# Two heads' last key tiles in one 256-column score product: a pre-norm block of segmented memory attention and GEGLU on one Trainium2 core

## The chip, the cores and the metric

The kernel runs as one program on one core of a Trainium2 chip. The metric is the time of one execution on the device in microseconds (us), the median of several runs; lower is better. The core's engines work side by side, each through its own queue in program order: TensorE (PE: matrix products, with the weight loads as a row of their own, PEld), VectorE (DVE), ScalarE (ACT), GpSimd (POOL), and SyncE (SP), which here issues all DMAs. An instruction waits in its engine's queue until the semaphores it names are set, and whatever stands behind it waits too. The matrix products write into eight accumulation banks in PSUM, each 128 partitions by 512 float32.

## What is computed

A transformer block over 2048 rows of 512 features, in float32: layer norm, attention in four segments of 512 rows with a compressive memory between the segments, residual, layer norm, GEGLU feed-forward (inner width 1376), residual. There are 32 heads of width 16.

```python
phi = lambda t: jnp.where(t > 0, t + 1.0, jnp.exp(t))
for s in range(N):                                  # N = 4 segments of L = 512 rows
    qs, ks, vs = q[:, :, s], k[:, :, s], v[:, :, s]
    logits = jnp.einsum("bhqd,bhkd->bhqk", qs, ks) * scale + mask
    p = _softmax(logits, axis=-1)
    a_dot = jnp.einsum("bhqk,bhkd->bhqd", p, vs)
    pq = phi(qs)
    num = jnp.einsum("bhld,bhde->bhle", pq, M)
    den = jnp.einsum("bhld,bhd->bhl", pq, z)[..., None] + 1e-6
    outs.append(g * (num / den) + (1.0 - g) * a_dot)
    pk = phi(ks)
    M = M + jnp.einsum("bhld,bhle->bhde", pk, vs)
    z = z + jnp.einsum("bhld->bhd", pk)
...
h = x + _A_ref(_layernorm(x, axis=-1), A_wq, A_wk, A_wv, A_wo, A_beta)
h2 = h + _B_ref(_layernorm(h, axis=-1), B_w_gate, B_w_up, B_w_down)   # (gelu(g) * u) @ w_down
```

The mask adds -1e9 where the key's index is below the query's, so each query attends to itself and to later keys of its segment. In the transposed scores (keys on partitions, queries along the columns) key tile `kb` of 128 keys needs the queries from `kb*128` on in the kernel's order of tiles: 512, 384, 256 and 128 columns for `kb` 0 to 3.

## The kernel before

**A planner writes the order.** The kernel's text describes operations with an engine, a modelled duration, the values they read and write (`Val`) and a due number `prio`. `Sched.run` simulates the five queues with these durations and a table of latencies between engines (`LAT`), takes at each step the operation that can start first (among those within 0.059 us the lowest `prio`), gives it buffers from pools, and emits its instructions. So the order in every queue is fixed when the program is built, and it follows from the modelled durations and from the table `DUE`, which shifts the due numbers of each unit's stages by up to four steps either way. A pool (`Pool_`) passes its buffers on to the pool named by `then` when nobody waits for them any more; `fifo=True` serves its values in the order of their creation.

**Attention.** A unit is a pair of a chunk of eight heads and a segment, 16 in all; each has two halves of four heads, so there are 32 passes `Q`. A product in full float32 precision is made of three products of split operands (`SPLIT`): a high part in float32r and the rest. `qkv` projects queries and keys (L576), splits them, and DMAs scatter the parts into stacks: `stq` (128 partitions, head pair `p`, 512 queries) and `stk` (128 partitions, `p`, `a`, 512 keys). Two heads share a pair `p`; head `a` of the two has its own 64 partitions in `stk[:, p, a]`, and the other 64 partitions are zero, so that one product over 128 partitions gives the scores of one head. `pass_a` computes scores with queries on partitions (L754), and the row maxima from them on VectorE (L764); these go by a DMA (L792, `stq<-mx`) into a row of `stq`, and with it a product of stacks gives scores less their maximum. `pass_b` computes the transposed scores (L809), the exponentials on ScalarE (L813), sets the masked triangle to zero on GpSimd (L817, `affine_select`), and multiplies by the values (L838, `accum`, four heads side by side in the array).

In `pass_b` the function `bank(parts)` fills one score bank with the parts `(head, column, key tile)`, runs one exponential over all 512 columns and the selections. A pass has ten banks: four heads with key tile 0 (512 columns), four heads with key tiles 1 and 3 (384 and 128 columns), and two banks with key tile 2 of two heads each. `accum` is called twice, for key tiles (0, 1) and (3, 2). The score banks are two (`PB`), the probabilities' buffers ten (`pt1` and `pt`).

**Start.** `ln1(0)` loads four row tiles, takes statistics (L483), an inverse square root by three Newton steps on VectorE (L488 to L499, twelve small instructions), normalizes four tiles (L504), transposes them on PE (L530, chunk by chunk of the features) and splits them (L539 on ScalarE, L540 on VectorE). Seventeen transposes of the last raw row tile (L555) keep PE at work before. `c_stk` fills the stacks with ones and zeros (L411 on ScalarE, L414 on GpSimd).

**Feed-forward.** It runs over two halves of the rows, `p` = 0 and 1, each 1024 rows as two sets of 512. The products are formed by a Strassen scheme of seven (`ffn`, L1082), whose operands `B[p]` come from `ln2` on both sets; `down` multiplies by the down weights (L1143). `B[p]` has fourteen operand tiles from the pool `PBL`, and those of the second half take over those of the first. For `B[1]` the rows are loaded again (L1189) into `PROW`, a pool of four row buffers that both sets use.

Of the kernel before, what the change touches and what calls it, by code (L numbers as in the profile page):

```python
# [242 lines left out]
def infini_geglu(ctx: ExitStack, tc: tile.TileContext, x, wq, wk, wv, wo, beta,  # L243
# [29 lines left out]
    def dma(prio, fn, ins, outs, kb=256, dur=None, **k):  # L273
        return S.op("SP", dur or (0.4 if kb == 256 else 0.64), prio, fn, ins, outs, lat=kb / 290, **k)
# [28 lines left out]
    PSQ = Pool_(stq_t, fifo=True, then=Parts(1, PBL, PBL, Parts(2, *[PHH] * 2), Parts(2, *[PHH] * 2)))  # L303
    PHL = Pool_(slots("hl", 3), fifo=True, then=Parts(1, FIN, Parts(2, *[PHH] * 2), Parts(2, *[PHH] * 2)))
    PROW = Pool_(many("row", 4, [P, D]), fifo=True)
    PRAW = Pool_(many("raw", 3, [P, D]), fifo=True)
# [7 lines left out]
    PPQ = Pool_(many("pq", 2, [P, D]), then=PC)  # L314
# [16 lines left out]
    PLN = Pool_(many("ln", 6, [P, 4]))  # L331
# [51 lines left out]

    vone, vq0, vk0, vv0 = Val(), [Val() for _ in stq_t], [Val() for _ in stk_t], [Val() for _ in va_t]
# [6 lines left out]
    def c_fill():  # L391
        for i, t in enumerate(stq_t):
            pool(0.93, -4.2 + 0.1 * i, lambda t=t: nc.gpsimd.memset(t.bitcast(F32), 0.0),
                 [vcalm[0]] if i > 1 else [], [vq0[i]])
# [53 lines left out]
    def layer_norm(prio, rows, dst, off=False, keep=None, acq=None, done=(), behind=(), scratch=None):  # L448
# [15 lines left out]
        def m_():  # L464
            return sc.t[:, 8:12] if scratch else mv.t[:, :, 0]
# [775 lines left out]
```

## Time and profile before

| | |
|---|---|
| runs (median, lowest to highest) | 847.04 us, 844.33 to 847.7 |
| the profiled execution, its span | 844.19 us, 842.5 us |
| mean granted clock of TensorE | 0.994 |
| instructions in the span | 15436 |
| DMA traffic in the span | 103.52 MB, mean 123 GB/s |

The span goes from the first to the last instruction; the time of the execution has some 1.7 us around it. The profile gives for each engine the time in which at least one of its instructions was under way; matrix products are pipelined, so their durations overlap (a single product of 512 columns is shown with about 0.4 us, though they follow each other faster). Groups of instructions are named by line, engine, operation and `out<-in` with the names of the buffers. As buffers are passed on between pools, a name tells where a buffer was first used, not what it holds: `stk` in the feed-forward stage is an operand tile. In the rows of the timeline stand the start, the length, what was done how often, and in brackets the idle time before it with what ended it.

### The profile page before, as it was taken

The numbers are of one execution on the slowest core, as the hardware profiler recorded it, in microseconds if no ns is written. First come the engines' busy times: TensorE is split into PE (matmuls) and PEld (weight loads), VectorE is DVE, ScalarE is ACT, GpSimd is POOL, SyncE is SP. The second block draws the span as 40 slices with busy tenths as digits, with TensorE's granted clock in tenths as the row PEclk, the third lists the DMA queues.
The fourth block names the chain that finished last, engine by engine and source line by source line (L and its number), as shares of the span: only waits on it lengthen the run. The fifth ranks groups of instructions, "written<-read, shape, count | busy, mean of one in ns | idle before, by whom it ended". The sixth has DMA issues, their size and how long they took to land.

```text
span 842.5 us, 15436 instructions
## 1 busy us (share of the span) xinstructions
PE 815.5 (97%) x4773; PEld 636.7 (76%) x4773; DVE 614.6 (73%) x1847; ACT 511.3 (61%) x966; POOL 493.9 (59%) x813
## 2 busy tenths in 40 slices
PE   5999999999999999999899999999999999999998
PEld 4887686776777777867576677878888777887886
DVE  7877789787976877769987864665567887656565
ACT  6765657678865656663675752684467664645551
POOL 6433436444444544545656895897696666778750
PEclk9999999999999999999999999999999999999999
DMA  6435445556456565356454654421113611212102
GB/s 225 113 97 141 133 132 144 162 162 170 124 139 177 138 182 136 104 152 194 131 177 141 217 182 146 127 86 53 54 57 100 209 45 38 65 49 63 50 1 100
DMA packets 71750, 103.52 MB, mean 123 GB/s; under 512 B 14324, under 2 KB 24884, under 8 KB 71668
## 3 DMA queue, kind: packets, MB, share of 16 engines
q1 hardware_dynamic: 71668, 102.54, 41.8%
q8 instruction: 38, 0.62, 0.3%
q14 instruction: 44, 0.36, 0.2%
HBM read 54.92 MB, written 21.43 MB: 91 GB/s over the span
## 4 chain that ended last, share of the span: by engine, by line
PE 84%; DVE 6%; POOL 3%; DMA 2%; issue 2%; ACT 2%; SPq 0%; POOLq 0%; DVEq 0%; ACTq 0%
PE bank L1082 22%; PE bank L1143 13%; PE bank L576 9%; PE bank L754 9%; PE bank L809 9%; PE bank L838 8%; PE bank L605 5%; PE bank L910 5%; DVE junk L764 2%; PE bank L683 1%; PE bank L729 1%; PE bank L530 1%; POOL raw L1059 1%; DMA row<-x 1%; DMA stq<-mx 1%
## 5 line engine op out<-in xcount | busy, mean ns | idle before, releaser
L764 DVE CUSTOM_DVE_ANT_0 junk<-bank,amask 128x384 f32<-128x384 f32 (+3 forms) x512 | 227.7, 486 | 46.2 <-PE bank L754 44.0
L813 ACT ACTIVATE pt<-bank 128x512 f32<-128x512 f32 x320 | 177.7, 599 | 58.8 <-PE bank L809 49.5
L817 POOL TENSOR_SCALAR_AFFINE_SELECT pt<-pt 128x128 f32<-128x128 f32 (+1 forms) x448 | 130.2, 311 | 139.2 <-ACT pt L813 133.6
L754 PE MATMUL bank<-stk,stq 128*128 128x512 f32 (+2 forms) x384 | 128.8, 387 | 1.1 <-DVE nm L764 0.7
L809 PE MATMUL bank<-stq,stk 128*128 128x384 f32 (+3 forms) x512 | 118.9, 324 | 3.1 <-DMA stq<-mx 1.5
L576 PE MATMUL bank<-xt,w 128*128 128x512 f32 x384 | 110.0, 398 | 2.0 <-DVE xt L540 2.0
L809 PEld LDWEIGHTS bank<-stq,stk 128*128 128x128 f32 x512 | 86.3, 190 | 20.1 <-ACT pt L813 7.2
L1148 DVE TENSOR_TENSOR pt<-pt,bank 128x512 f32<-128x512 f32 x96 | 65.0, 686 | 35.1 <-PE bank L1143 34.7
L754 PEld LDWEIGHTS bank<-stk,stq 128*128 128x128 f32 x384 | 67.4, 189 | 24.3 <-DVE nm L764 8.1
L576 PEld LDWEIGHTS bank<-xt,w 128*128 128x128 f32 x384 | 68.1, 188 | 13.0 <-DVE xt L540 2.2
L838 PE MATMUL bank<-pt,vaug 128*32 128x512 f32 (+3 forms) x1024 | 76.7, 436 | 0.0
L838 PEld LDWEIGHTS bank<-pt,vaug 128*32 128x32 f32 x1024 | 28.4, 109 | 36.5 <-issue 30.6
L605 PE MATMUL bank<-wv,xt 128*128 128x256 f32 x384 | 54.9, 283 | 0.0
L605 PEld LDWEIGHTS bank<-wv,xt 128*128 128x128 f32 x384 | 52.5, 189 | 2.4 <-DVE xt L540 0.2
L427 POOL TENSOR_TENSOR w<-raw,w 128x512 fp32r<-128x512 f32 (+1 forms) x26 | 33.7, 1298 | 31.1 <-ACT w L422 28.3
L1082 PE MATMUL bank<-xt,w 128*128 128x512 f32 (+1 forms) x180 | 51.7, 402 | 0.0
L1082 PE MATMUL bank<-xt,stk 128*128 128x512 f32 (+1 forms) x156 | 44.5, 398 | 2.1 <-POOL xt L950 1.5
L879 POOL TENSOR_TENSOR n<-n,r 128x512 f32<-128x512 f32 x16 | 21.0, 1311 | 40.3 <-DMA r<-r_dram 32.6
L858 ACT ACTIVATE pvs<-bank 128x512 f32<-128x512 f32 x32 | 19.1, 598 | 40.5 <-PE bank L838 24.1
L764 DVE DVE_READ_ACCUMULATOR2_ANT nm<- 128x1 f32 x512 | 42.2, 82 | 0.0
L1052 POOL TENSOR_TENSOR w<-raw,w 128x512 fp32r<-128x512 f32 (+2 forms) x33 | 38.0, 1154 | 4.9 <-ACT w L1050 4.8
L1052 POOL TENSOR_TENSOR stk<-raw,stk 128x512 fp32r<-128x512 f32 (+3 forms) x30 | 35.0, 1170 | 9.8 <-ACT stk L1050 9.2
(297 smaller groups left out, 1745.7 us busy)
## 6 DMA issues: line engine op xcount, KB each, us to landing
stq<-hl SPq DMA_DIRECT2D x96, 128.0 KB
stk<-hl SPq DMA_DIRECT2D x192, 64.0 KB
pv_dram<-pvs SPq DMA_DIRECT2D x32, 256.0 KB
r<-r_dram SPq DMA_DIRECT2D x28, 256.0 KB
row<-x SPq DMA_DIRECT2D x24, 256.0 KB
raw<-wg SPq DMA_DIRECT2D x20, 256.0 KB
raw<-wu SPq DMA_DIRECT2D x20, 256.0 KB
raw<-wd SPq DMA_DIRECT2D x20, 256.0 KB
```

What stands on the lines that cost most here:

```text
L576: nc.tensor.matmul(pm.t, w.t[:, wi, dc * P:(dc + 1) * P], XT[s][dc].t[:, xi, :], start=dc == 0 and n == 0, stop=dc == ND - 1 and n == 2)
L605: nc.tensor.matmul(pm.t[:, 256 * t:256 * t + 256], XT[s][dc].t[:, xi, t0:t0 + P], whl[wi].t[:, h, 256 * (dc % 2):256 * (dc % 2) + 256], st ...
L754: nc.tensor.matmul(sa.t[:, k * w:(k + n) * w].rearrange("x (n w) -> x n w", n=n), sq.t[:, p, i * P:(i + 1) * P], sk.t[:, p, a:a + n, 0:w], ...
L764: nc.vector.tensor_tensor_reduce(out=junk.t[:, :w], in0=sa.t[:, k * w:(k + 1) * w], in1=amask[:, D - w:], op0=OP.add, op1=OP.min, scale=-1 ...
L809: nc.tensor.matmul(sc.t[:, lo:lo + D - q0], sk.t[:, p, a, q0:q0 + P], sq.t[:, p, q0:D], start=True, stop=True)
L813: act(D, prio, lambda: nc.scalar.activation(e.t, sc.t, AF.Exp), [sc], [e])
L817: nc.gpsimd.affine_select(v, v, pattern=pat + [[1, P]], compare_op=OP.is_ge, fill=0.0, base=0, channel_multiplier=-1)
L838: nc.tensor.matmul(pv.t[32 * n:32 * n + 32, kb * P:D], va.t[:, kb, 17 * j:17 * j + 32], e.t[:, lo:lo + D - kb * P], start=kb == 0, stop=la ...
L1052: pool(0.14 + 2.13e-3 * (hi - lo), prio, lambda: nc.gpsimd.tensor_tensor(v.t[:, 1, :hi - lo], r.t[:, lo:hi], v.t[:, 0, :hi - lo].bitcast(F ...
L1082: nc.tensor.matmul(dst.t[:w], v.t[:, wi, c0 + j * w:c0 + (j + 1) * w], b[bk][j].t[:, xi, :], start=first and j == 0 and n == 0, stop=j == ...
L1143: nc.tensor.matmul(pm.t, HH[p, f, s][hi].t[:w, t * P:(t + 1) * P], v.t[:w, wi, :], start=f == fl[0] and n == 0, stop=f == fl[-1] and n == 2)
L1148: dve(D, prio, lambda a=a, pm=pm: nc.vector.tensor_tensor(a.t, a.t, pm.t, op=OP.add), [pm], [a])
```

## The change

Eight edits are made together.

1. In `pass_b`, ScalarE copies the last 128 keys and queries of the pass from the stacks into small stacks: `k3` holds both heads' own 64 partitions in one tile, `q3` has a head's queries in its own 64 partitions and zeros in the others. One product of 256 columns for a pair then gives the last key tile of two heads, and one bank holds it for all four heads.
2. So a pass has eleven banks: four of 512 columns, four of 384, one of four times 128, two of twice 256. The exponential runs over the columns in use only. `accum` is called for (0, 1, 3) and for (2,).
3. `layer_norm`'s three Newton steps become one step of higher order and one Newton step (nine instructions become seven). In `ln1(0)` the fourth row tile is normalized on ScalarE, the transposes go row by row, all four banks in one operation, and the warm-up transposes read the statistics in place of the last row.
4. The second stack's fill waits for the first split chunk `XT[0][0]`.
5. The second row set of `B[1]` gets buffers of its own: `PROW2` takes the two `r` and the two `om` buffers when attention is done with them. The feed-forward pool `PGE`, which had them before, is left with three buffers.
6. One more `pt1` buffer, one `pq` buffer less, two more `ln` buffers, and new tiles `k3` (one) and `q3` (two, zeroed at the start).
7. Modelled durations: small DMAs 0.68 in place of 0.64 us, gathering reads as if of 430 KB in place of 256.
8. All of `DUE` is new, so the order in every queue is laid out anew.

```diff
-    "q": [0.25, 2.625, -4, 1, -1.25, 1.375, -0.625, -4, 0.25, -1.25, 2.125, 0.75, 0, 0.875, 0, 1.125],
+    "q": [-2.625, -0.25, 3.5, 2.5, 1.75, 1.625, -0.25, 0.875, 0.375, 0.625, 1.75, 1.75, 1.75, 1.625, 3.5, 1],
...
-        return S.op("SP", dur or (0.4 if kb == 256 else 0.64), prio, fn, ins, outs, lat=kb / 290, **k)
+        return S.op("SP", dur or (0.4 if kb == 256 else 0.68), prio, fn, ins, outs, lat=kb / 290, **k)
...
+    k3_t = many("k3", 1, [P, 2, P], F32R)
+    q3_t = many("q3", 2, [P, 2, 2, P], F32R)
+    PK3, PQ3 = Pool_(k3_t, fifo=True), Pool_(q3_t, fifo=True)
...
+    PROW2 = Pool_([], fifo=True)
...
-    PROW1 = Pool_(many("pt1", 8, [P, D]), then=PPT)
+    PROW1 = Pool_(many("pt1", 9, [P, D]), then=PPT)
...
-    PR = Pool_(many("r", 2, [P, D]), then=PGE)
+    PR = Pool_(many("r", 2, [P, D]), then=PROW2)
...
-    POM = Pool_(many("om", 2, [P, D]), then=PGE)
+    POM = Pool_(many("om", 2, [P, D]), then=PROW2)
...
+        for i, t in enumerate(q3_t):
+            pool(0.5, -3.8 + 0.1 * i, lambda t=t: nc.gpsimd.memset(t.bitcast(F32), 0.0),
+                 [vcalm[0]], [vz3[i]])
...
+            pe(17 * 0.227, prio, lambda: [nc.tensor.transpose(
+                wm.t[0:24, 0:P], bn.t.rearrange("p t k -> p (t k)"), ident) for n in range(17)],
+                [bn, vident], [wm])
...
+        steps = [(stt(u_, v_, 1.0, y_, OP.mult, OP.mult), [v, y], [u]),
+                 (stt(z_, u_, 1.0, y_, OP.mult, OP.mult), [u, y], [z]),
+                 (stt(u_, z_, -10.0 / 3.0, z_, OP.add, OP.mult), [z], [u]),
+                 (stt(y_, u_, 5.0, y_, OP.add, OP.mult), [u, y], [y]),
+                 (stt(u_, v_, -0.5 * F ** 3, y_, OP.mult, OP.mult), [v, y], [u]),
+                 (stt(u_, u_, 1.0, y_, OP.mult, OP.mult), [u, y], [u]),
+                 (stt(y_, u_, 1.5 * F, y_, OP.add, OP.mult), [u, y], [y])]
...
+            if b:
+                act(4, prio, lambda: nc.scalar.activation(
+                    rows[3].t, rows[3].t, AF.Identity, scale=y.t[:, 3:4], bias=b.t[:, 3:4]),
+                    [b, y], [rows[3]])
...
+            pe(4 * TR, prio, lambda: [nc.tensor.transpose(
+                pts[dc].t[:, t * P:(t + 1) * P], rows[t].t[:, dc * P:(dc + 1) * P], ident)
+                for t in range(4) for dc in range(ND)], [*rows, vident], pts, acq=dst)
...
-            wm = Val(PB)
-            pe(17 * 2 * TR, prio, lambda: [nc.tensor.transpose(
-                wm.t[:, (n % 4) * P:(n % 4 + 1) * P], rows[3].t[:, (n % 4) * P:(n % 4 + 1) * P],
-                ident) for n in range(17)], [rows[3], vident], [wm])
...
+        k3, q3 = Val(PK3), Val(PQ3)
+        zeros = vz3[Q:Q + 1]
+        for a in range(2):
+            own = slice(64 * a, 64 * a + 64)
+            act(2 * P, prio, lambda a=a, own=own: nc.scalar.activation(
+                k3.t[own], sk.t[own, :, a, 3 * P:], AF.Copy), [sk], [k3], src=0.22, chain=True)
+            act(2 * P, prio, lambda a=a, own=own: nc.scalar.activation(
+                q3.t[own, :, a], sq.t[own, :, 3 * P:], AF.Copy), [sq, mr] + zeros, [q3], src=0.22, chain=True)
...
+                if kb == 3:
+                    for p in range(2):
+                        nc.tensor.matmul(
+                            sc.t[:, 2 * P * p:2 * P * p + 2 * P].rearrange("x (a q) -> x a q", a=2),
+                            k3.t[:, p], q3.t[:, p], start=True, stop=True)
+                    return
...
-            act(D, prio, lambda: nc.scalar.activation(e.t, sc.t, AF.Exp), [sc], [e])
+            act(w, prio, lambda: nc.scalar.activation(e.t[:, :w], sc.t[:, :w], AF.Exp), [sc], [e])
...
         for n in range(4):
-            bank([(n, 0, 1), (n, 3 * P, 3)])
-        accum((0, 1), False)
+            bank([(n, 0, 1)])
+        bank([(n, n * P, 3) for n in range(4)])
+        accum((0, 1, 3), False)
         for n in range(2):
             bank([(n, 0, 2), (n + 2, 2 * P, 2)])
-        accum((3, 2), True)
+        accum((2,), True)
...
-        for first, ap, kb in ((16 * D, [32, 16], 24), (0, [D, 16], 256)):
+        for first, ap, kb in ((16 * D, [32, 16], 24), (0, [D, 16], 430)):
...
-    c_stk(1, [vcalm[0]])
+    c_stk(1, [vcalm[0], XT[0][0]])
...
-                    rows = [Val(PROW) for _ in range(4)]
+                    rows = [Val(PROW2 if s else PROW) for _ in range(4)]
```

More of the change, by code (lines that the diff above doesn't have):

```diff
@@ L330, in infini_geglu @@
     PMV = Pool_(many("mv", 2, [P, 4, 2]))
-    PLN = Pool_(many("ln", 6, [P, 4]))
+    PLN = Pool_(many("ln", 8, [P, 4]))
     ident = sb("ident", [P, P])
@@ L379, in infini_geglu @@
     vcalm = [Val(), Val()]
+    vz3 = [Val() for _ in q3_t]
     vone, vq0, vk0, vv0 = Val(), [Val() for _ in stq_t], [Val() for _ in stk_t], [Val() for _ in va_t]
@@ L464, in m_ @@
         def m_():
-            return sc.t[:, 8:12] if scratch else mv.t[:, :, 0]
+            return sc.t[:, 8:12] if scratch and off else mv.t[:, :, 0]
         for t in range(4):
@@ L485, in layer_norm @@
                 dve(840, prio, f, [rows[t], *behind], [bn, mv], chain=True)
+        if done and not behind:
+            wm = Val(PB)
+            pe(17 * 0.227, prio, lambda: [nc.tensor.transpose(
+                wm.t[0:24, 0:P], bn.t.rearrange("p t k -> p (t k)"), ident) for n in range(17)],
+                [bn, vident], [wm])
         def g():
@@ L505, in norm, with bias @@
                                         op0=OP.subtract, op1=OP.mult)
-            dve(3700, prio, lambda: [*[f() for f in [g, *steps]], *[norm(t) for t in range(4)]],
-                [mv, *rows, *(HL0 if behind else [])], [v, u, y, *rows, *done])
+            n = 4 if behind else 3
+            b = None if behind else Val(PLN)
+            def bias():
+                nc.vector.scalar_tensor_tensor(b.t, m_(), -1.0, y.t, op0=OP.mult, op1=OP.mult)
+            dve(3500 if behind else 3250, prio, lambda: [
+                *[f() for f in [g, *[f for f, _, _ in steps], *([bias] if b else [])]],
+                *[norm(t) for t in range(n)]],
+                [mv, *rows, *(HL0 if behind else [])], [v, u, y, z, *([b] if b else []), *rows[:n], *done])
+            if b:
+                act(4, prio, lambda: nc.scalar.activation(
+                    rows[3].t, rows[3].t, AF.Identity, scale=y.t[:, 3:4], bias=b.t[:, 3:4]),
+                    [b, y], [rows[3]])
         else:
             dve(400, prio, g, [mv], [v, u, y])
-            for i, f in enumerate(steps):
-                dve(4, prio, f, [v, y] if i % 3 == 0 else [u, y], [u] if i % 3 < 2 else [y])
+            for f, ins, outs in steps:
+                dve(4, prio, f, ins, outs)
         if off:
@@ L524, in layer_norm @@
                     op1=OP.mult), [rows[t], mv, y], [rows[t]])
+        if done and not behind:
+            pts = [Val(PA if dc == 3 else PD) for dc in range(ND)]
+            pe(4 * TR, prio, lambda: [nc.tensor.transpose(
+                pts[dc].t[:, t * P:(t + 1) * P], rows[t].t[:, dc * P:(dc + 1) * P], ident)
+                for t in range(4) for dc in range(ND)], [*rows, vident], pts, acq=dst)
+            for dc in range(ND):
+                split_psum(prio, pts[dc], dst[dc])
+            return
         for dc in range(ND):
-            pt = Val(PA if done and dc == 3 and not behind else PD)
+            pt = Val(PD)
             def tr(dc=dc, pt=pt):
@@ L810, in f @@
                                      sq.t[:, p, q0:D], start=True, stop=True)
-            pe(sum(mm(D - kb * P) for _, _, kb in parts), prio, f, [sq, sk, mr], [sc],
-               acq=[e], tail=mm(D - parts[-1][2] * P))
-            act(D, prio, lambda: nc.scalar.activation(e.t, sc.t, AF.Exp), [sc], [e])
-            step = parts[1][1] if len(parts) > 1 else 0
+            if kb == 3:
+                pe(2 * mm(2 * P), prio, f, [k3, q3], [sc], acq=[e], tail=mm(2 * P))
+            else:
+                pe(len(parts) * mm(D - kb * P), prio, f, [sq, sk, mr], [sc], acq=[e],
+                   tail=mm(D - kb * P))
+            act(w, prio, lambda: nc.scalar.activation(e.t[:, :w], sc.t[:, :w], AF.Exp), [sc], [e])
             def keep(v, pat):
@@ L820, in g @@
             def g():
-                if step == 2 * P:
-                    keep(e.t.rearrange("p (b q) -> p b q", b=2)[:, :, 0:P], [[0, 2]])
-                else:
-                    for d0 in ([0, step] if step else [0]):
-                        keep(e.t[:, d0:d0 + P], [])
-            pool(0.25 if not step else 0.36 if step == 2 * P else 0.49, prio, g, [e], [e])
+                if len(parts) == 1:
+                    keep(e.t[:, 0:P], [])
+                else:
+                    v = e.t.rearrange("p (b q) -> p b q", b=len(parts))
+                    keep(v[:, :, 0:P], [[0, len(parts)]])
+            pool((0.25, 0.36, 0, 0.6)[len(parts) - 1], prio, g, [e], [e])
             for n, lo, kb in parts:
```

25 lines of the change are left out of this document (15 added, 10 removed), and 33 rows, old and new, of the table DUE.

## The prediction

> **What bounds the kernel now.** I read the busy shares first, then the busy time by stage, then the waits of TensorE (PE), and last the timelines of three places.
>
> ```profile
> PE 815.5 (97%) x4773; PEld 636.7 (76%) x4773; DVE 614.6 (73%) x1847; ACT 511.3 (61%) x966; POOL 493.9 (59%) x813
> ```
>
> ```profile
> core 0: us, PE busy (x) PEld busy (x) DVE busy (x) ACT busy (x) POOL busy (x), PEclk, DMA share, GB/s
> 0.00:15.49 15.49, 6.61 (x34) 5.35 (x34) 11.31 (x36) 8.21 (x12) 9.36 (x21) 1.00 0.75 256
> 15.49:467.90 452.41, 443.81 (x3118) 336.76 (x3118) 361.12 (x1420) 298.43 (x575) 220.34 (x539) 1.00 0.52 145
> ```
>
> The second fence is the table by stretches: length, then each engine's busy time. In the attention stage (15.49 to 467.90) PE is busy for 443.8 of 452.4 us, so no other engine's work counts there unless it makes PE wait, and only 8.6 us of idling could be won back. What is left is PE's own work, the start (8.9 us of PE idle), and the change from the first to the second half of the rows in the feed-forward stage (PE idles 3.3 us of these 22):
>
> ```profile
> 660.00:682.00 22.00, 18.73 (x82) 14.73 (x81) 18.87 (x42) 14.04 (x25) 11.77 (x13) 0.92 0.61 194
> ```
>
> Then who PE waited for in the whole execution (total, times, longest), of which two rows matter later.
>
> ```profile
> PE bank L809 <- DMA stq<-mx: 1.5, 2, 1.1
> ...
> PE bank L809 <- ACT pt L813: 1.4, 4, 0.6
> ```
>
> The score products (L809) wait for ScalarE's exponentials only 1.4 us in all. So the sum is: PE work removed, plus stalls removed at the two places, minus PE waits that ScalarE's new work makes.
>
> **The 128-column products.** Each of the 32 passes multiplies four last key tiles of 128 columns; the change does them in two products of 256. The question is what 128 columns cost on PE. The page's busy times overlap, so I go by starts in PE's timeline (start, length, count).
>
> ```profile
> 265.98 0.40 PE L809 MATMUL bank<-stq,stk 128*128 128x384 f32 x2
> 266.21 0.44 PE L754 MATMUL bank<-stk,stq 128*128 128x512 f32 x1
> 266.49 0.40 PE L809 MATMUL bank<-stq,stk 128*128 128x384 f32 x2
> 266.73 0.39 PE L754 MATMUL bank<-stk,stq 128*128 128x384 f32 x1
> 266.96 0.86 PE L576 MATMUL bank<-xt,w 128*128 128x512 f32 x3
> ```
>
> ```profile
> 20.38 0.88 PE L605 MATMUL bank<-wv,xt 128*128 128x256 f32 x6
> 21.09 0.86 PE L576 MATMUL bank<-xt,w 128*128 128x512 f32 x3
> 21.79 5.19 PE L605 MATMUL bank<-wv,xt 128*128 128x256 f32 x42
> ```
>
> ```profile
> 655.16 2.20 PE L1082 MATMUL bank<-xt,w 128*128 128x512 f32 x9
> ```
>
> 256 columns: (5.19 - 0.88)/36 = 0.120 us. 512 columns: nine in 2.20, three in 0.86, so 1.34/6 = 0.22. Between them 384 columns are 0.17. Each "x2" of L809 is one product of 384 and one of 128. From 265.98 to 266.96 there pass 0.98 us; three products of 384 and one of 512 take 0.73 to 0.75 of it; 0.23 to 0.25 remain for two of 128: 0.12 each, as much as one of 256. Per pass 4 x 0.12 becomes 2 x 0.12; 32 passes save 32 x 0.24 = **7.7 us** of PE.
>
> The Trainium skill, "TensorE: Matmul & The Clock Gate", section Back-to-back issue gap, speaks against this: an isolated warm product costs its columns at 2.4 GHz plus 2.5 ns, so 128 columns would be 56 ns and 256 columns 109 ns. By that rule this term would be nothing; the row above gives twice its 56 ns, and I go by the row.
>
> **What ScalarE gets for it.** Four copies of 256 elements per pass build the small stacks, and the exponentials go from ten of 512 to seven of 512 and four of 384.
>
> ```profile
> L813 ACT ACTIVATE pt<-bank 128x512 f32<-128x512 f32 x320 | 177.7, 599 | 58.8 <-PE bank L809 49.5 <-POOL pt L817 8.1 <-POOL n L881 0.6
> ```
>
> The nearest rows for the copies:
>
> ```profile
> L616 ACT ACTIVATE vaug<-bank 128x256 f32<-128x256 f32 x32 | 10.8, 383 | 18.4 <-PE bank L605 18.3
> ...
> L1050 ACT ACTIVATE w<-raw 128x256 fp32r<-128x256 f32 x9 | 3.7, 411 | 1.7 <-DMA raw<-wu 1.0 <-PE bank L1143 0.7
> ```
>
> ```profile
> 185.40:199.60 14.20, 14.20 (x104) 10.56 (x103) 11.32 (x46) 12.60 (x27) 5.67 (x16) 1.00 0.65 175
> ```
>
> A copy on 64 partitions from two slices is not in the trace. Its bounds are 0.38 (L616) and 0.60 (512 elements, L813); I take 0.41, the row of a 256-element copy from SBUF. From 0.383 and 0.599, 384 elements take 0.49, so the exponentials go from 5.99 to 7 x 0.599 + 4 x 0.49 = 6.15. Per pass that is 1.64 + 0.16 = 1.8 us, in all 58 us, and ScalarE's share of the stage rises from 298/452 = 66% to 356/445 = 80%. On average there is room beside PE. In the fullest stretch of one pass's length (the last row, 12.60 of 14.20) 1.8 more makes 14.4: it doesn't fit, and exponentials come late, which hold the two score banks. The layout is new throughout and can spread this, or not. I charge **+2.0 us**; the ends are 0 (all hidden) and about 7 (1.8 in each of four full stretches). GpSimd gets three selections fewer per pass, and one wider; with 220 of 452 us busy it gains nothing that PE sees. The second weighted-sum group now needs only key tile 2; the first needs one bank more. Work is the same, so nothing.
>
> The new order can also keep or lose the 8.6 us of idling in this stage, either way by some 4 us; that goes into the range.
>
> **The start.**
>
> ```profile
> 7.46 0.17 DVE L488 TENSOR_SCALAR bank<-mv 128x4 f32<-128x4 f32 x1
> ...
> 9.87 1.91 DVE L504 TENSOR_SCALAR pt<-pt,mv,ln 128x512 f32<-128x512 f32 x4
> ...
> 13.19 1.04 ACT L411 ACTIVATE stk<-one 64x1024 fp32r<-64x1024 f32 x1
> ...
> 14.14 2.02 ACT L539 ACTIVATE xt<-bank 128x512 fp32r<-128x512 f32 x4
> ```
>
> ```profile
> 6.62 3.86 PE L555 MATMUL bank<-ident,pt 128*128 128x128 f32 x17 [6.62 <-DMA pt<-x]
> 10.48 3.00 PE L530 MATMUL bank<-ident,pt 128*128 128x128 f32 x16
> 15.49 5.05 PE L576 MATMUL bank<-xt,w 128*128 128x512 f32 x21 [2.01 <-DVE xt L540]
> ```
>
> The twelve small steps run from 7.46 to 9.87, 0.20 each. Ten and the bias step end at 9.67, three rows on VectorE at 0.48 each end at 11.1, and the fourth goes to ScalarE beside them. But the 17 warm-up transposes now start after the statistics, at about 7.5 (the first step that reads them starts at 7.46), and at their 3.86 us end at 11.4. They, and not the rows, then hold the 16 transposes, which at 0.11 each (twelve in 1.47, below) end at 13.1; all four banks are complete only then, since the order is now by row. The copies L539 were held to 14.14 by a fill of a stack (13.19, 1.04 us); that fill now waits for the first copy and with its second half (another 1.04) and GpSimd's zeros comes after. So they start at about 13.4 and the first product at 14.7 in place of 15.49: **-0.8 us**. Ends: 0, if another ScalarE step stands in front, and 2.0, the whole idle. Behind the moved fill wait the DMAs that scatter the second pass's keys; they follow the whole first pass's in SP's queue, which covers it, so I charge nothing (up to 1 us, the length of one half of the fill, if that cover is gone). Two more zero fills on GpSimd are hidden too.
>
> **The change of halves.**
>
> ```profile
> 641.41 1.75 SPq L1189 DMA_DIRECT2D row<-h_dram  x4
> ```
>
> ```profile
> 669.53 1.47 PE L530 MATMUL bank<-ident,row 128*128 128x128 f32 x12
> 672.74 0.66 PE L530 MATMUL bank<-ident,row 128*128 128x128 f32 x4 [1.74 <-DVE pq L939]
> ...
> 675.43 0.74 PE L1082 MATMUL bank<-xt,stk 128*128 128x512 f32 x2 [1.53 <-POOL xt L950]
> ```
>
> ```profile
> 676.00:679.50 3.50, 3.50 (x10) 2.69 (x9) 3.43 (x7) 1.94 (x4) 3.10 (x3) 0.55 0.00 0
> ```
>
> The second row set is loaded at 641.41, when the first set's transposes have given its four buffers back; its own come 28 us later, the last in PE's queue before it idles 1.74 and 1.53 us. Then the clock is at 0.55 for 3.5 us (the last row, PEclk): another 1.6 lost. Together 4.9. With four buffers of its own (PROW2, free since the attention stage) the set can load with the first one. The four loads leave SP's queue at 641 and stand in it earlier, among weight loads that run far ahead. What is late next are the tiles of the first half's operands, which the new ones take over; the nine products at 655.16 (above) are already the new half's, so the old ones are read by then, 14 us ahead of 669.5. The cost: the feed-forward activations keep three buffers of seven, for two in use at a time. I take **-4.0 us**, with ends 0 and -4.9.
>
> The same page of the Trainium skill, section Why this matters for your kernels, puts the fall of the clock at idle gaps over about 3 us. Here the longest gap is 1.74 and the clock falls nevertheless. By the rule the 1.6 would stay and the term be -2.4 at most.
>
> **Sum.** The profiled execution took 844.2 (its span is 842.5). 844.2 - 7.7 + 2.0 - 0.8 - 4.0 = 833.7. The three timed runs have 844.3, 847.0 and 847.7; the median is 2.8 above the profiled one. I put the forecast half of that above the sum: **835.0 us**.
>
> **Rivals.**
>
> 1. Nothing saved on PE: a product of 128 costs half of one of 256. For it: nothing but the formula above; against it: the 0.98 us of six products. Without the 7.7: 841.4, with the 1.4 about 842.8.
> 2. ScalarE fills up: 7 in place of 2.0. For it: 12.60 of 14.20 busy; against it: 1.4 us of such waits now. About 840.
> 3. The halves stay unmended, because another wait of the chain (a PSUM bank for its statistics) sets it: 839.
> 4. Slower: the stack's query copy stands in ScalarE's queue and waits for the DMA of the row maxima, and the exponentials of the pass before wait behind it.
>
> ```profile
> 207.37 0.73 PE L809 MATMUL bank<-stq,stk 128*128 128x512 f32 x2 [1.11 <-DMA stq<-mx]
> ```
>
> Such a landing made PE wait 1.11 here. Before, PE alone waited, twice in 32 passes; now ScalarE would too. It decides from 12.5/32 = 0.39 us in each pass. At 0.6 the time is 844.2 - 12.5 + 19.2 = 850.9, with the 1.4 about 852. Against it: the copies are needed only by the ninth of eleven banks, so they can stand late.
>
> **How the numbers follow.** Forecast 0.55; rival 1 0.11; rival 2 0.13; rival 3 0.12; rival 4 0.09. A measurement can tell about 0.5%, 4.2 us, from no change: faster is below 842.8. The forecast and rival 3 lie below it nearly always, rival 2 in two of three cases, rival 1 in less than half: faster 0.77, same 0.14, slower 0.09. The range goes from 826 (all of the start and of the change of halves, no ScalarE charge, some 4 us of idling won back) to 845 (rivals 1 to 3 with their spread); rival 4 lies outside.
>
> **What would show it.** 256-column products of L809's successor 0.12 apart; PE's busy time in the attention stage some 7 lower; the first 512-column product before 15; no granted clock under 0.9 near 670, and the second row load long before 641; ScalarE's share in the stage near 80% and PE's waits for exponentials under 4 us. I am wrong if PE idles for ScalarE, or for the copies' DMA, in most passes.

## The result, and the profile after

| | before | changed |
|---|---|---|
| median of the runs, us | 847.14 | 831.72 |
| lowest to highest, us | 844.33 to 847.7 | 829.82 to 833.6 |
| profiled execution, its span, us | 844.19, 842.5 | 830.79, 829.1 |
| instructions in the span | 15436 | 15346 |

The changed kernel is faster: the ratio of the times is 0.9836, with a 95% interval of 0.9809 to 0.9863. The forecast was 835.0 and its sum for the profiled execution 833.7; that execution took 830.79. The next views are of single executions, the one of each kernel that was profiled.

First the busy shares on the page of the changed kernel.

```profile
span 829.1 us, 15346 instructions
...
PE 805.0 (97%) x4709; PEld 623.6 (75%) x4709; DVE 612.0 (74%) x1831; ACT 563.5 (68%) x1127; POOL 484.2 (58%) x719
```

PE is busy for 10.5 us less than before, with 64 products fewer, and is still the bound. ScalarE has 52.2 us more. Next the table by stretches of the changed kernel (length, then busy time of each engine, granted clock, DMA share, GB/s): the start, the attention stage, and the change of halves.

```profile
0.00:14.02 14.02, 5.33 (x34) 4.06 (x34) 10.31 (x32) 7.45 (x10) 8.95 (x20) 1.00 0.86 298
14.02:463.20 449.18, 439.08 (x3058) 328.53 (x3059) 363.09 (x1412) 351.48 (x738) 213.67 (x451) 1.00 0.53 146
...
660.00:671.00 11.00, 11.00 (x50) 9.13 (x49) 4.88 (x8) 3.60 (x7) 5.56 (x7) 1.00 0.82 268
671.00:680.00 9.00, 9.00 (x42) 7.33 (x41) 6.62 (x11) 6.77 (x13) 8.21 (x9) 1.00 0.33 104
```

The first product comes at 14.02 in place of 15.49. ScalarE has 351.5 of 449.2 us, 78%, where 80% was foreseen. From 660 to 680, where PE idled 1.74 and 1.53 us and then ran at half clock, it is now busy throughout at full clock. In the attention stage PE is busy for 439.08 us, 4.7 less than before, and idle for 10.1 where it idled 8.6. The waits of PE (total, times, longest), first one row of before, then the changed kernel:

```profile
PE bank L754 <- DVE nm L764: 0.7, 3, 0.3
```

```profile
PE bank L797 <- DVE nm L807: 3.9, 8, 0.8
PE bank L869 <- ACT pt L876: 1.4, 3, 0.5
...
PE bank L862 <- ACT pt L876: 0.7, 2, 0.4
```

L869 is the old L809, and L862 the new product of 256 columns: the score products wait 2.1 us for exponentials, against 1.4 before. The wait that grew most is another: L797, the old L754, waits 3.9 us for VectorE's row maxima, where it waited 0.7.

To see which part of the kernel gave the 13.4 us of span, I cut each execution at one point of its work: where about 1200 of the 1644 products of the feed-forward and the output product are still to come. This lies in the feed-forward stage, after the last attention pass and ahead of the change of halves. The table has the start of the first 512-column product too, and the time up to the point in which the granted clock stood at 0.50.

| kernel | first product, us | up to the point, us | of it at clock 0.50, us | from there to the end, us |
|---|---|---|---|---|
| before | 15.49 | 553.6 | 6.8 | 288.9 |
| changed | 14.02 | 545.7 | 0 | 283.4 |
| changed, four products of 128 (first run below) | 14.24 | 553.3 | 3.4 | 283.4 |
| the same without the copies (second run) | 14.15 | 552.2 | 6.8 | 283.4 |
| changed without the copies (third run) | 15.03 | 545.2 | 0 | 283.8 |
| changed, one row pool (fourth run) | 15.31 | 548.2 | 0 | 288.7 |
| before, two row pools (fifth run) | 15.27 | 554.5 | 6.8 | 281.2 |

The stretches at clock 0.50 come from rows like these, two of before, then one of the first run and one of the second:

```profile
417.00:420.40 3.40, 3.30 (x10) 2.72 (x11) 3.40 (x18) 1.42 (x3) 1.64 (x3) 0.50 0.59 171
468.20:471.60 3.40, 3.40 (x14) 3.00 (x15) 0.50 (x1) 2.18 (x5) 3.40 (x5) 0.50 0.00 0
```

```profile
468.50:471.90 3.40, 3.40 (x18) 3.07 (x22) 0.95 (x2) 2.46 (x5) 1.39 (x3) 0.50 0.00 0
```

```profile
464.80:471.60 6.80, 6.46 (x26) 4.86 (x30) 3.58 (x8) 4.84 (x10) 2.68 (x8) 0.50 0.11 40
```

So 5.5 us were gained behind the point, where the change of halves lies, and 7.9 ahead of it. Of the 7.9, 1.5 lie ahead of the first product; half the clock for 6.8 us costs 3.4; 3.0 are left. From the first product to the point, with the clock's loss taken out, before needs 534.7 us, the changed kernel 531.7, and the first three runs below 537.4, 534.7 and 530.2. The experiments take these apart.

### The profile page after: what moved, and what is told of

It reads as the page before. It is cut to its first block, busy times and chain, and to the rows that moved or that the text cites. A ratio compares the mean times of both kernels' runs of the same rounds, so it can differ in the third digit from the quotient of the medians.

```text
span 829.1 us, 15346 instructions
## 1 busy us (share of the span) xinstructions
PE 805.0 (97%) x4709; PEld 623.6 (75%) x4709; DVE 612.0 (74%) x1831; ACT 563.5 (68%) x1127; POOL 484.2 (58%) x719
## 4 chain that ended last, share of the span: by engine, by line
PE 77%; DVE 10%; ACT 4%; issue 3%; POOL 3%; DMA 2%; SPq 1%; ACTq 0%; POOLq 0%; DVEq 0%
PE bank L1145 19%; PE bank L1206 14%; PE bank L619 8%; PE bank L797 8%; PE bank L869 7%; PE bank L900 7%; PE bank L973 4%; PE bank L648 4%; DVE junk L807 3%; ACT pt L876 1%; PE bank L726 1%; POOL raw L1122 1%; PE bank L772 1%; PE bank L579 1%; DVE hl L682 1%
## 5 line engine op out<-in xcount | busy, mean ns | idle before, releaser
L807 DVE CUSTOM_DVE_ANT_0 junk<-bank,amask 128x256 f32<-128x256 f32 (+3 forms) x512 | 228.3, 485 | 43.4 <-PE bank L797 40.3
L879 POOL TENSOR_SCALAR_AFFINE_SELECT pt<-pt 128x128 f32<-128x128 f32 (+2 forms) x352 | 118.8, 346 | 191.6 <-ACT pt L876 183.5
L876 ACT ACTIVATE pt<-bank 128x512 f32<-128x512 f32 (+1 forms) x352 | 181.4, 560 | 42.8 <-PE bank L869 36.4
L797 PE MATMUL bank<-stk,stq 128*128 128x512 f32 (+2 forms) x384 | 128.1, 377 | 4.3 <-DVE nm L807 3.9
L869 PE MATMUL bank<-stq,stk 128*128 128x384 f32 (+2 forms) x384 | 110.8, 351 | 1.7 <-ACT pt L876 1.4
L797 PEld LDWEIGHTS bank<-stk,stq 128*128 128x128 f32 x384 | 68.6, 188 | 28.4 <-DVE nm L807 13.8
L869 PEld LDWEIGHTS bank<-stq,stk 128*128 128x128 f32 x384 | 67.3, 188 | 19.9 <-ACT pt L876 8.3
L648 PEld LDWEIGHTS bank<-wv,xt 128*128 128x128 f32 x384 | 52.2, 189 | 1.8 <-issue 0.2
L1115 POOL TENSOR_TENSOR w<-raw,w 128x512 fp32r<-128x512 f32 (+3 forms) x37 | 42.0, 1137 | 6.8 <-ACT w L1113 6.6
L1145 PEld LDWEIGHTS bank<-xt,w 128*128 128x128 f32 (+1 forms) x186 | 34.3, 186 | 8.9 <-ACT ge L1163 0.8
L1145 PE MATMUL bank<-stk,w 128*128 128x512 f32 (+1 forms) x138 | 38.8, 390 | 0.0
L1122 POOL TENSOR_TENSOR raw<-raw,raw 128x256 f32<-128x256 f32 (+1 forms) x44 | 35.2, 799 | 2.9
L1122 POOL TENSOR_TENSOR raw<-raw 128x256 f32<-128x256 f32 (+1 forms) x44 | 33.6, 765 | 1.8
```

The source lines that it names most:

```text
L648: nc.tensor.matmul(pm.t[:, 256 * t:256 * t + 256], XT[s][dc].t[:, xi, t0:t0 + P], whl[wi].t[:, h, 256 * (dc % 2):256 * (dc % 2) + 256], st ...
L797: nc.tensor.matmul(sa.t[:, k * w:(k + n) * w].rearrange("x (n w) -> x n w", n=n), sq.t[:, p, i * P:(i + 1) * P], sk.t[:, p, a:a + n, 0:w], ...
L807: nc.vector.tensor_tensor_reduce(out=junk.t[:, :w], in0=sa.t[:, k * w:(k + 1) * w], in1=amask[:, D - w:], op0=OP.add, op1=OP.min, scale=-1 ...
L869: nc.tensor.matmul(sc.t[:, lo:lo + D - q0], sk.t[:, p, a, q0:q0 + P], sq.t[:, p, q0:D], start=True, stop=True)
L876: act(w, prio, lambda: nc.scalar.activation(e.t[:, :w], sc.t[:, :w], AF.Exp), [sc], [e])
L879: nc.gpsimd.affine_select(v, v, pattern=pat + [[1, P]], compare_op=OP.is_ge, fill=0.0, base=0, channel_multiplier=-1)
```

## The experiments

In each, "before" and "changed" name the two kernels, and medians are compared with those of runs on the same chip where there are any.

**1. Four products of 128 columns in the new order.** All else stays, the copies too: the last key tile is multiplied from the large stacks again.

```diff
-                if kb == 3:
-                    for p in range(2):
-                        nc.tensor.matmul(
-                            sc.t[:, 2 * P * p:2 * P * p + 2 * P].rearrange("x (a q) -> x a q", a=2),
-                            k3.t[:, p], q3.t[:, p], start=True, stop=True)
-                    return
...
-                pe(2 * mm(2 * P), prio, f, [k3, q3], [sc], acq=[e], tail=mm(2 * P))
+                pe(2 * mm(2 * P), prio, f, [k3, q3, sk, sq], [sc], acq=[e], tail=mm(2 * P))
```

> The changed kernel with its order in every queue kept, but the last key tiles as four products of 128 columns from the large stacks. The small stacks are still copied; nobody reads them. Theory A (a product of 128 costs PE as much as one of 256, 0.12 us): 32 x 2 x 0.12 = 7.7 us more than the changed kernel, 839 to 840. Theory B (a product of 128 costs half, and the gain of the change comes from the new order, which has no long stalls near 415 and 467): within 1 us of the changed kernel, 831 to 833.

Measured: 837.5 us (835.35 to 839.22), ratio to before 0.9871 (0.9833 to 0.9908). That is 5.8 above the changed kernel, and 5.9 above the third run, which was on the same chip as this one. The table above puts it wholly ahead of the point (553.3 against 545.7, of which 1.7 went to the clock). In the timeline of PE in this run (start, length, count), four products of 128 stand between one of 384 and a group of another line:

```profile
251.03 0.34 PE L797 MATMUL bank<-stk,stq 128*128 128x384 f32 x1
251.21 0.56 PE L863 MATMUL bank<-stq,stk 128*128 128x128 f32 x4
251.60 0.93 PE L648 MATMUL bank<-wv,xt 128*128 128x256 f32 x6
```

From 251.21 to 251.60 there pass 0.39 us: 0.10 for each. In the changed kernel two products of 256 columns stand in the same way between others:

```profile
54.34 0.40 PE L862 MATMUL bank<-q,k 128*128 128x256 f32 x2
54.57 0.40 PE L869 MATMUL bank<-stq,stk 128*128 128x256 f32 x2
```

They take 0.23 us, 0.12 each. So a pass saves 0.16 us, and 32 passes 5.1. Added up over all 32 passes, waits within them included, the four products take 14.2 us and the two 9.4: 4.8 less.

**2. The same without the copies.** The copies' two calls become `lambda: None`; nothing in this kernel reads the small stacks.

```diff
-            act(2 * P, prio, lambda a=a, own=own: nc.scalar.activation(
-                k3.t[own], sk.t[own, :, a, 3 * P:], AF.Copy), [sk], [k3], src=0.22, chain=True)
+            act(2 * P, prio, lambda: None, [sk], [k3], src=0.22, chain=True)
...
```

> As the run before, and the four copies of a pass are left out too, with ScalarE's waits for the maxima's DMA; the order of all else is that of the changed kernel. Theory A with copies that PE hardly feels: within 1 us of the run before. Copies that cost PE what the prediction charged: 2 us less than the run before, about 837.5; 5 to 7 less if ScalarE is the bound in its full stretches.

Measured: 836.57 us (834.9 to 837.24), ratio 0.9854 (0.9815 to 0.9894): 0.9 below the first run, with overlapping ranges.

**3. The products of 256 columns without the copies.** The changed kernel with the same edit; the small stacks are set to zero once, so the kernel leaves out the scores of the last key tiles.

> The changed kernel with its 256-column products and its order kept, but the four copies of a pass left out: the products read small stacks that were zeroed once at the start, so the scores of the last key tiles are zero. Copies hidden: 831 to 832, no change. Copies charged as predicted: 2 us less, about 829.7. ScalarE the bound in full stretches: 825 to 827.

Measured: 831.59 us (830.71 to 832.89), ratio 0.9803 (0.977 to 0.9837). Against the changed kernel's 831.72 the copies cost 0.1 us; against the second run the products alone give 5.0. With four executions each, whose ranges overlap by about 2 us, the medians can't tell the forecast 2.0 for the copies from nothing. The executions profiled say more: from the first product to the point, with the clock's loss taken out, the copies cost 1.5 us here (531.7 - 530.2) and 2.7 with the four products (537.4 - 534.7); the joined products give 4.5 without the copies (534.7 - 530.2) and 5.7 with them (537.4 - 531.7). In the groups of the changed kernel (line, form, count, busy time, mean ns, idle time before and what ended it) one sees what they take of ScalarE:

```profile
L849 ACT ACTIVATE k<-stk 64x256 fp32r<-64x256 f32 x64 | 26.4, 413 | 2.4 <-PE bank L862 0.7 <-DMA stk<-hl 0.7
L851 ACT ACTIVATE q<-stq 64x256 fp32r<-64x256 f32 x64 | 26.3, 411 | 10.4 <-DMA stq<-mx 9.8
L876 ACT ACTIVATE pt<-bank 128x384 f32<-128x384 f32 x128 | 58.1, 494 | 18.9 <-PE bank L869 17.3 <-POOL pt L879 0.7
```

A copy takes 0.41 us and an exponential of 384 columns 0.49, as forecast. L851 shows the wait of the fourth rival: ScalarE stands idle for the DMA of the row maxima for 9.8 us in all. It does so in front of the query copies. How much of this is in the 1.5 to 2.7 us that the copies cost, the runs don't separate.

**4. One row pool in the changed kernel.**

```diff
-                    rows = [Val(PROW2 if s else PROW) for _ in range(4)]
+                    rows = [Val(PROW) for _ in range(4)]
```

> The changed kernel with both row sets of the second half in the four buffers of PROW again; the order is the same up to the change of halves and laid out anew behind it. If the second pool mends that place: 4 to 6 us more, 836 to 838, with a PE stall of some 3 us and a granted clock near a half there. If another wait sets it (rival 3): within 1 us.

Measured: 837.84 us (835.82 to 838.6), ratio 0.9872 (0.9838 to 0.9907), 6.1 above the changed kernel. By the table 5.3 us of span come back after the point and 2.5 ahead of it, 1.3 of these in front of the first product, where the edit changes nothing. The stretches of this run, and PE's waits in it:

```profile
660.00:668.00 8.00, 6.26 (x35) 5.15 (x33) 5.51 (x11) 5.85 (x11) 4.07 (x6) 1.00 0.97 308
668.00:676.00 8.00, 6.76 (x19) 4.96 (x20) 7.87 (x13) 5.59 (x10) 6.09 (x6) 0.57 0.15 55
...
668.90:675.72 6.82, 5.59 (x13) 4.18 (x13) 6.69 (x12) 4.41 (x9) 5.26 (x5) 0.50 0.05 18
```

```profile
PE bank L579 <- DVE e L1002: 1.7, 1, 1.7
PE bank L1145 <- POOL xt L1013: 1.2, 1, 1.2
```

In its timeline of SP the four row loads come together and late again:

```profile
636.72 1.75 SPq L1252 DMA_DIRECT2D row<-h_dram  x4
```

Both stalls are back in their old places: PE starts again at 667.98 after 1.74 us and at 670.49 after 1.23. The clock is at 0.50 from 668.9 to 675.7, that is from between the two on.

**5. Two row pools in before.** Edit 5 alone.

```diff
+    PROW2 = Pool_([], fifo=True)
...
-    PR = Pool_(many("r", 2, [P, D]), then=PGE)
+    PR = Pool_(many("r", 2, [P, D]), then=PROW2)
...
-    POM = Pool_(many("om", 2, [P, D]), then=PGE)
+    POM = Pool_(many("om", 2, [P, D]), then=PROW2)
...
-                    rows = [Val(PROW) for _ in range(4)]
+                    rows = [Val(PROW2 if s else PROW) for _ in range(4)]
```

> The kernel before with edit 5 alone (PROW2 for the second row set, three buffers left for PGE); the order is that of before up to the second half's row loads. If that place is mended by the pool alone: 4 to 5 us less than before, without the stalls of 1.74 and 1.53 us and the half clock at 676. If PGE's buffers or another wait gives it back: within 1 us of before.

Measured: 838.56 us (837.58 to 841.16), ratio to before 0.9913 (0.9892 to 0.9933). The point is reached at 554.5 in place of 553.6, and the rest takes 7.7 us less. The stretches of before, and then those of this run:

```profile
560.00:575.00 15.00, 14.34 (x64) 11.55 (x63) 8.88 (x17) 9.32 (x16) 12.42 (x12) 1.00 0.26 71
...
650.00:690.00 40.00, 36.73 (x161) 29.54 (x160) 32.72 (x66) 27.82 (x53) 23.67 (x24) 0.96 0.42 132
```

```profile
560.00:575.00 15.00, 15.00 (x67) 12.11 (x66) 13.48 (x43) 12.42 (x24) 14.84 (x14) 1.00 0.19 54
...
650.00:690.00 40.00, 40.00 (x177) 32.52 (x176) 28.12 (x46) 20.91 (x39) 26.73 (x29) 1.00 0.47 147
```

From 650 to 690 PE idled 3.3 us and lost 4% of 40 us, 1.6, to the clock: the 4.9 of the forecast, and all of it is gone. The other 2.8 lie elsewhere behind the point: 0.66 us of idling from 560 to 575 (15.00 - 14.34) is gone as well, and a wait of 0.51 at 700.5; PE doesn't wait at all behind the point in this run. What became of the last 1.6 I did not follow. The changed kernel, with the same two pools, needs 2.2 us more from the point on (283.4 against 281.2), and there PE still waits three times, 1.2 us in all, near 560 and at 721. Of the two edits that were tried alone on before (4 and 5) this is the one that brings a gain.

**6. The second stack's fill later, in before.** Edit 4 alone, with the due time that lets the fill stand behind the copies.

```diff
-    c_stk(1, [vcalm[0]])
+    c_stk(1, [vcalm[0], XT[0][0]], -2)
```

> The kernel before with the wait of the second stack's fill alone (edit 4); in the queues only ScalarE's two fills and GpSimd's two zero fills move, two places and one. If the fill held the first copies: the first 512-column product starts at about 14.0 in place of 15.49, and about 1.5 us less in all. If the layer norm's edits give the start's gain: 15.4 to 15.5, no change.

Measured: 848.05 us (845.35 to 849.73), ratio 1.0012 (0.999 to 1.0034). The copies did not come earlier. ScalarE's timeline in this run:

```profile
12.25 0.63 ACT L469 ACTIVATE junk<-row 128x512 f32<-128x512 f32 x1 [2.92 <-DMA row<-x]
...
13.32 0.72 ACT L478 ACTIVATE junk<-row,bn 128x512 f32<-128x512 f32 x1 [0.34 <-DVE bn L475]
...
14.04 2.04 ACT L539 ACTIVATE xt<-bank 128x512 fp32r<-128x512 f32 x4
15.95 2.12 ACT L411 ACTIVATE stk<-one 64x1024 fp32r<-64x1024 f32 x2
```

The fill is behind the copies, as wished, and a second step of the next row set's statistics (L478) has taken its place; the first (L469) stood ahead of the copies already. The copies start at 14.04 in place of 14.14.

**7, 8 and 9. Other orders.** The kernel's planner was given other numbers in `DUE`: for before with about the same planned end (7), for the changed kernel with one 0.3 us earlier (8), and for before with one 2.0 us earlier (9).

> The kernel before with other due numbers, all edits left out; its planner gives 824.2 for it, 823.9 for before. If the order alone carries what edits 1, 4 and 5 leave unexplained (2 to 4 us of stalls and half clock near 415 and 468): it differs from before by 2 us or more either way. If order matters little at an equal planned end: within 1.5 us.

> The changed kernel with due numbers searched further by its own planner, which gives 809.7 in place of 810.0. If the chip follows the planner: within 1 us of the changed kernel, 831 to 832.5. If the order decides at random within some us: outside 829.5 to 834.

> The kernel before, none of the edits, with due numbers searched further by its own planner (821.9 in place of 823.9; its planned waits of PE near 410 are gone). If the 1.93 us stall at 415 with the half clock behind it, which all four profiled kernels of the old order have and none of the new order has, comes from the order of the queues: that stall is under 1 us here, no half clock at 417, and the time is 2 to 3.5 us less than before, 844 to 845.5 where before has 847. If the stall belongs to what the edits remove: it stays at 1.9 and the time is within 1 us of before.

Measured: 847.24 (ratio 1.0002, 0.9989 to 1.0014), 833.24 (0.9847, 0.9827 to 0.9866) and 846.25 us (0.998, 0.9961 to 0.9999). No order that I tried moved either kernel by more than 1.7 us. The third was meant to explain a stretch in which before loses some 2 to 3 us that the forecast doesn't count. The rows of before, then of the third order:

```profile
412.00:419.00 7.00, 4.55 (x27) 2.79 (x24) 7.00 (x27) 2.02 (x5) 5.32 (x5) 0.86 0.48 139
419.00:426.00 7.00, 6.97 (x43) 5.25 (x45) 6.80 (x21) 5.94 (x12) 3.66 (x13) 0.90 0.51 151
```

```profile
412.00:419.00 7.00, 3.88 (x40) 1.83 (x29) 7.00 (x17) 2.69 (x5) 6.61 (x9) 0.89 0.34 95
419.00:426.00 7.00, 7.00 (x40) 5.71 (x39) 5.15 (x14) 4.37 (x9) 2.70 (x9) 0.63 0.51 146
```

And the changed kernel:

```profile
412.00:419.00 7.00, 6.17 (x54) 3.77 (x54) 6.89 (x23) 3.22 (x7) 1.85 (x3) 1.00 0.55 140
```

VectorE is full in all three. In before PE idles 2.4 us of seven and then loses clock; in the third order it idles 3.1 and loses more clock; the changed kernel idles 0.8 and keeps the clock. So these two other orders of before didn't mend it, and my theory that before's own order was the cause fell.

**10, 11 and 12. The start.** The changed kernel with its transposes by feature chunk, as before has them (10); with one warm-up transpose in place of 17 (11); and as it is, again on the same chip (12).

```diff
-                for t in range(4) for dc in range(ND)], [*rows, vident], pts, acq=dst)
+                for dc in range(ND) for t in range(4)], [*rows, vident], pts, acq=dst)
```

```diff
-                wm.t[0:24, 0:P], bn.t.rearrange("p t k -> p (t k)"), ident) for n in range(17)],
+                wm.t[0:24, 0:P], bn.t.rearrange("p t k -> p (t k)"), ident) for n in range(1)],
```

> The changed kernel with the sixteen transposes of the first row set written by feature chunk, so that a bank is complete after four of them and not after thirteen; nothing else in any queue moves. If the first bank releases ScalarE's copies (and not the whole set): the copies start at about 12.0 in place of 12.64 and the first 512-column product at about 13.4 in place of 14.02; some 0.6 us less in all than the changed kernel. If the set as a whole releases them: 14.0, no change.

> The changed kernel with one warm-up transpose in place of seventeen, all else in order. If the warm-up's end does not hold the start (the rows do): the sixteen transposes start at 11.0 to 11.3 as now but at 0.21 us each, the first 512-column product comes 0.7 to 1.7 later, and a stretch of products behind it runs at half clock: 2 to 3.5 us more than the changed kernel. If the warm-up is not needed for the clock: within 0.5 us.

> The changed kernel once more, beside the two runs before it on the same chip: 830 to 834 us, first 512-column product at 14.0.

Measured: 831.14 (830.21 to 831.7; ratio 0.9824, 0.9795 to 0.9853), 832.54 (831.82 to 835.2; 0.9844, 0.9815 to 0.9873) and 831.85 us (831.2 to 832.88; 0.9831, 0.9807 to 0.9856). The three can't be told apart by their times. PE's and ScalarE's timelines tell more; first the changed kernel, PE and then ScalarE:

```profile
7.61 3.58 PE L497 MATMUL bank<-ident,bn 128*24 128x128 f32 x17 [7.61 <-DVE bn L491]
11.02 1.91 PE L568 MATMUL bank<-ident,pt 128*128 128x128 f32 x16
14.02 5.75 PE L619 MATMUL bank<-xt,w 128*128 128x512 f32 x24 [1.08 <-DVE xt L589]
```

```profile
12.64 2.07 ACT L588 ACTIVATE xt<-bank 128x512 fp32r<-128x512 f32 x4 [1.91 <-PE bank L568]
```

By chunk, PE and then ScalarE:

```profile
11.56 2.91 PE L568 MATMUL bank<-ident,pt 128*128 128x128 f32 x16
14.23 5.75 PE L619 MATMUL bank<-xt,w 128*128 128x512 f32 x24
```

```profile
12.66 0.60 ACT L588 ACTIVATE xt<-bank 128x512 fp32r<-128x512 f32 x1 [1.55 <-PE bank L568]
```

With one warm-up transpose, PE:

```profile
10.38 3.56 PE L568 MATMUL bank<-ident,pt 128*128 128x128 f32 x16 [2.42 <-DVE pt L533]
...
14.83 5.54 PE L619 MATMUL bank<-xt,w 128*128 128x512 f32 x23 [0.89 <-DVE xt L589]
```

From the start of the transposes to the copies there pass 1.62 us by row (12.64 - 11.02) and 1.10 by chunk (12.66 - 11.56): by row the copies do wait longer, but not for all sixteen. In the changed kernel the thirteenth transpose, the last into the first bank, ends at 12.61 and the first copy starts at 12.64; in run 12 it is 13.25 and 13.29.

The starts of the transposes in these traces tell why the executions differ. The warm-up's follow each other at 0.21 us, and from some point on those behind them at 0.11. That point is at 10.8 us in the changed kernel (the last of the warm-up), at 12.2 in run 12, and at 13.5 in run 10 and in the fourth run; in run 11 all sixteen are 0.21 apart. The first product goes with it: 14.02, 14.67 and, in the fourth run, 15.31 by row; 14.23 in run 10, by chunk; 14.83 in run 11. So the warm-up's worth isn't shown: the kernels that have it and the row order start at 14.02 to 15.31, the one without at 14.83. What the order by row costs is: where the spacing is 0.21, the copies start 2.78 us behind the first transpose by row (13.94 - 11.16, fourth run) and 1.10 by chunk.

## Why the prediction was right, and where its terms were off

The direction, the range and three of the four mechanisms held; the sizes did so less well. By terms, in us:

| term | forecast | measured |
|---|---|---|
| products of 128 columns | -7.7 | -4.5 to -5.8 |
| ScalarE's copies and exponentials | +2.0 | +0.1 and +0.9 by medians, +1.5 and +2.7 in the executions profiled (the copies) |
| start, first product | -0.8 | -1.5; -0.2 to -1.3 in four other executions with the same start |
| change of halves | -4.0 | -5.3 to -5.5; -7.7 by the pools alone in before |
| not counted: clock 0.50 near 417 and 468 | 0 | -3.4 |

**The products.** The mechanism was right and the size too large. I had 0.12 for a product of 128 columns, from a remainder of 0.23 to 0.25 us shared by two; four in a row take 0.39, 0.10 each, and two of 256 take 0.23. So 0.16 us a pass were saved where I had 0.24. The sign that I had named, some 7 us less of PE's busy time in the attention stage, came out as 4.7. The first rival (nothing saved) fell. What I set against the row is the formula that the Trainium skill ("TensorE: Matmul & The Clock Gate", section Back-to-back issue gap) gives for an isolated product: 56 ns for 128 columns. The same section of the Trainium skill says that this counts too little for small products that each load their weights, and gives about 81 ns for them; the run has 98, above both. The formula's 109 ns for 256 columns is near the 0.12 us measured.

**ScalarE.** The durations and the share were right (0.41, 0.49; 78% for 80%). Whether the charge was is open: the medians give less, the executions profiled about as much. The argument for it was wrong. The stretch with 12.60 us was the fullest of the rows that I had, not of the stage: 190.97 to 205.17 of before has 13.73. And the changed kernel has a full one with PE busy throughout:

```profile
170.00:184.20 14.20, 14.20 (x101) 10.93 (x100) 11.06 (x49) 13.16 (x30) 7.30 (x18) 1.00 0.64 191
```

The score products' waits for exponentials rose by 0.7 us only, and the second rival (840) fell. The fourth rival's wait is real, 9.8 us of ScalarE's time, but 0.31 us a pass (9.8/32), below the 0.39 that I had given as its point of decision.

**The start.** The forecast lies within what the executions show, but two steps were wrong. I had the fill hold the copies L539; the sixth run moves the fill, and the copies start 0.1 us earlier, as other work of ScalarE stands in its place. And I had all four banks complete only with the last transpose, at 13.1; the thirteenth of the sixteen releases the first copy, at 12.64. That the warm-up and not the rows holds the transposes was right: without it, in run 11, they start at 10.38 in place of 11.02. I also took 0.11 us for each transpose, while in four of the executions told of above a part of them or all are 0.21 apart, and the first product moves with that. What remains unproved is which of edit 3's parts gives the gain: shorter statistics or the fourth row on ScalarE. The order by row doesn't.

**The change of halves.** The mechanism was right in each step: the second set's rows are loaded at 517 to 541, the stalls and the half clock are gone, and the fourth run brings them back. The timeline of SP in the changed kernel shows the new loads in the old `r` and `om` buffers among them:

```profile
517.26 0.42 SPq L1252 DMA_DIRECT2D r<-h_dram  x1
...
525.12 0.42 SPq L1252 DMA_DIRECT2D row<-h_dram  x1
525.59 0.42 SPq L1252 DMA_DIRECT2D om<-h_dram  x1
...
540.62 0.42 SPq L1252 DMA_DIRECT2D om<-h_dram  x1
```

I took 4.0 of an available 4.9, for no row of the trace; 5.3 to 5.5 came, and 7.7 in before, where smaller waits behind the point went too. The activation buffers that were given up cost nothing that shows in the fifth run. The clock, too, went the way of the row: it stood at 0.50 for 6.8 us in the fourth run, from 0.9 us behind a gap of 1.74 us on, and at 1.00 without the gap. So the 1.6 belonged to the term. By the Trainium skill's rule ("TensorE: Matmul & The Clock Gate", section Why this matters for your kernels) such a gap is too short to lower it; the fourth run disagrees. The third rival fell.

**The rest.** The profiled execution of before stands at clock 0.50 twice ahead of the point, which costs it 3.4 us; that of the changed kernel doesn't. Near 417 this goes with the structure: each profiled kernel with before's structure has a stall of 1.5 us or more at 415 to 420 and half clock behind it, and none of those with the changed structure has the half clock there. It isn't tied to a single edit, and runs 7 and 9 show that another order alone doesn't mend it. Near 468 it doesn't go with the structure: half clock stands between 462 and 475 in before and runs 5 and 7, not in 6 and 9, and in runs 1, 2 and 12 of the changed structure, not in the others. Run 12 is the changed kernel itself. So this half of the 3.4 us may be luck of the execution. The stage's idling, of which the range had "some 4 us" won back, rose by 1.5 us. The other new parts (edits 2, 3, 6 and 7 and the new order) were not tried one by one; together they changed nothing between first product and point, where before and the second run, with the products apart and no copies, both need 534.7 us.

**The sum.** Between the two executions profiled, the start gave 1.5 us (0.8 forecast), the joined products and the copies with all that lies between first product and point 3.0 (5.7 forecast: 7.7 less 2.0), the clock ahead of the point 3.4 (nothing forecast), and the part behind the point 5.5 (4.0 forecast): 13.4 in place of 10.5. That is the 2.9 us between 833.7 and 830.79. The step from there to the median was 1.4 and came out as 0.9 (831.72 - 830.79). So that the forecast missed by 3.3 us only is in part luck: the first edit gave 2.7 less than its two terms, and the clock ahead of the point, which I had not counted, gave 3.4.

No kernel that was run clearly beats the changed one: the transposes by chunk have 831.14 against 831.85 on the same chip, with overlapping ranges.

## What to carry to other kernels

When PE is the bound, count what its smallest products cost from start to start in its timeline, with what stands around them: here a product of 128 columns cost nearly as much as one of 256 (0.10 against 0.12 us), so two small ones were worth joining, even though the copies for it, on an engine with idle time, may have taken a third of the gain or more. Where a pool of buffers is shared by two sets that follow each other, look at when the loads leave their queue: buffers of their own, taken from work that is over, gave back 5 to 8 us of small stalls and of the half clock near them. Before two single executions are compared, take out what half clock and a later start put between them: here that was as large as some of the terms. And before a step is moved to free an engine, ask what the planner will put in its place.

## What had not been expected of the hardware

- The clock fell behind short gaps: to 0.50 for 6.8 us, from 0.9 us behind a wait of 1.74 us on, with PE busy for 6.26 of the 8 us from 660 to 668 (fourth run). In run 12 it fell to 0.50 at 462.8, where no wait was longer than 0.52 us; in the changed kernel's first execution the same waits left it at 1.00.
- The same transposes of the start took 1.91, 2.48, 2.91 and 3.56 us in four executions (runs: the changed kernel, 12, 10 and 11). The last had one warm-up transpose; the first three had the same 17, and of these only the third has another order of transposes. Within the executions that have the 17, the spacing of the transposes halves at one point, from 0.21 to 0.11 us, 2.9 to 5.9 us behind the first transpose of the warm-up; the granted clock in the rows is 1.00 before and behind it.
- The spread of the changed kernel's runs goes with the clock: 829.82 and 830.79 us at a mean clock of 1.000, 832.65 and 833.6 at 0.997 and 0.998.
